# Gated linear attention and two MoE layers on one core: batch row 0 of the attention in three tiles of 128 rows

## The chip, the core and the metric

The kernel runs on one NeuronCore of a Trainium2 chip. What counts is the device time of one launch in microseconds (us), the median of the runs. Engines: PE is TensorE, DVE is VectorE, ACT is ScalarE, POOL is GpSimd, SP is SyncE, which here only issues DMAs. Each engine works through its own list of instructions in order. Line numbers such as L613 are lines of the kernel before; a helper's line stands for everything that it issues.

## The reference, cut to what matters

```
# attention: B, H, S, D = 4, 8, 768, 48
for t in range(S):
    state = alpha[:, :, t, :, None] * state + einsum('bhd,bhe->bhde', k[:, :, t], v[:, :, t])
    y[:, :, t] = einsum('bhd,bhde->bhe', q[:, :, t], state)
x = y.transpose(0, 2, 1, 3).reshape(3072, 384)
# first MoE: the best of 8 experts for each token, 384 -> 1024 (relu) -> 384, times its gate
# second layer for all tokens: 384 -> 2048, h * sigmoid(h), -> 384
```

## The kernel before

The time axis of the attention (768 steps) is cut into 6 chunks of 128. Two heads form a pair; there are 16 pairs `p`, four for each of the 4 batch rows. On chip a pair's q, k and alpha lie with the feature on the partitions: head 0 on partitions 0 to 47, head 1 on 64 to 111, time along the row. Such a layout is a tile. In batch rows 1 to 3 the four pairs share three tiles of 128 partitions: pair `4b + 3` is cut into six pieces of 16 rows, and they lie in the gaps of the other three tiles, on partitions 48 to 63 and 112 to 127 (`ASIDE` says which piece goes where). Batch row 0 instead has four tiles of 112 partitions, one for each pair. So there are 13 tiles `T` (`NTL`).

Each tile is prepared by five steps (`prep`), once for all rows in it:

- `P_SCAN` (L562, output `Pf`): running products of alpha inside each chunk, a scan on DVE, and a small reciprocal (L565).
- `Q_SCALE` (L574): q times `Pf`, on POOL; for tile 0 alone on DVE.
- `DECAY` (L569): copies the chunk ends for the state scan, on ACT.
- `R_SCAN` (L580, output `Rv`): products from the chunk's end backwards, a scan on DVE.
- `K_SCALE` (L585): k times `Rv`, on DVE.

A pair then needs: `scores` (L607) for chunks 0 to 2 and 3 to 5 on PE into the same PSUM tile `Ap`, each half followed by a causal mask that moves it out as `Am` (L613 on DVE, or for some halves a copy on ACT at L626 and two selects on POOL at L630: `beside_scans`); transposes of k (`Tp`, copied to `kst` by ACT at L598); `updates` (L643, L650), which fill `U`; the state scan `So` (L660) on DVE; two copies of it to `Sb` on ACT (L679); and, a pair later, `from_states` (L690) and `within` (L702, L705), which build the output `Yp`, copied out by ACT (L719). The loop over `p` is written so that pair `p` goes with the outputs of pair `p - 1`, and `work` says beside which pair each preparing step stands: `P_SCAN` of a tile stands two pairs before the first pair that uses it, in front of the second half's mask; `R_SCAN` at the end of that same pair; `K_SCALE` at the head of the next. A pair of the kind `4b + 1` has no scans beside it in batch rows 1 to 3.

For the fourth pair of a batch row `gather_last` puts the six pieces together into the extra buffer `E_5` by six DMAs from chip memory to chip memory, issued by POOL. There are five ordinary buffers `E_0` to `E_4` for q and k, three for alpha (`a_`) and four for v.

All input loads are issued by SP. The framework hands out eight counters (`DMAHW0` to `DMAHW7`) in turn to the DMAs of SP and ACT together, and an issue waits until the earlier DMA of its counter has landed. A tile of batch row 0 takes one DMA for each of alpha, q and k; a tile of the others takes four (two of 48 rows, two of 16).

`warm(n)` issues `n` small matmuls of zeros on PE. After the attention the first MoE layer and the second layer follow, both bound by PE; the change does not touch them.

Of the kernel before, what the change touches and what calls it, by code (L numbers as in the profile page):

```python
# [21 lines left out]
B, H, S, D = 4, 8, 768, 48  # L22
NP = B * H // 2
PA = 112
CH = 128
NC = S // CH
SP = NC * (CH + 1)
# [212 lines left out]
def gla_moe_kernel(  # L240
# [12 lines left out]
    nc = tc.nc  # L253
# [151 lines left out]
    with actx:  # L405
# [9 lines left out]


        ASIDE = (((0, 16), (0, 32)), ((1, 0), (1, 16)), ((1, 32), (0, 0)))
        NTL = 4 + 3 * (B - 1)
        NE = 5


        Es = [ac.tile([128, 2 * S + D * NC], F32, name=f"E_{i}") for i in range(NE + 1)]
        tl = {}

        def place(T):
            if T < 4:
                return 0, T
            b, j = divmod(T - 4, 3)
            return b + 1, j

        def parts(e):
            return dict(
# [13 lines left out]
        def load(T, what="aqk"):  # L446
            if T >= NTL:
                return
            b, j = place(T)
            tl.setdefault(T, parts(Es[T % NE]))  # L450
            for x in what:
                src, t = load_to(T, x)
                n = src.shape[2]
                z = src[4 * b + j]
                if b:
                    z = [(0, z[0:D]), (64, z[64:PA])]
                    for i, (h, d) in enumerate(ASIDE[j]):
                        s0 = 64 * h + d
                        z.append((64 * i + D, src[4 * b + 3][s0 : s0 + 16]))
                    for r0, y in z:  # L460
                        nc.sync.dma_start(t[r0 : r0 + y.shape[0]], y)
                else:

                    for c0, c1 in ((0, SP // 2), (SP // 2, n)) if x == "a" and T == 0 else ((0, n),):
                        nc.sync.dma_start(t[0:PA, c0:c1], z[:, c0:c1])

        def load_v(p):
            if p < NP:
# [73 lines left out]
        def gather_last(b):  # L542

            for j in range(3):
                for i, (h, d) in enumerate(ASIDE[j]):
                    s0 = 64 * h + d
                    nc.gpsimd.dma_start(Es[NE][s0 : s0 + 16], Es[(3 * b + 1 + j) % NE][64 * i + D : 64 * i + 64])

        def begin(p):
            b, j = divmod(p, 4)  # L550
            e = Es[p if not b else NE if j == 3 else (3 * b + 1 + j) % NE]
            st.setdefault(p, {}).update(parts(e))

        def prep(T):
            s = tl[T]
            i = T % 2
            n = PA if T < 4 else 128

            def f0():
                s["Pf"] = wk.tile([128, SP], F32, tag="Pf", name="Pf", bufs=3)  # L560
# [58 lines left out]

        def beside_scans(p, g):  # L620

            return (p, g) == (NP - 2, 1) or g == 0 and 1 <= p <= 4

        def mask_aside(p, g):
            m = st[p]["m", g]
# [328 lines left out]
        def f(T, i):  # L954
            if T < NTL:
                if T not in prs:
# [6 lines left out]
        def at(p, place, T, *steps):  # L963
            if T < NTL:
                work.setdefault((p, place), []).extend((T, i) for i in steps)
# [48 lines left out]
        P_SCAN, Q_SCALE, DECAY, R_SCAN, K_SCALE = range(5)  # L1014
        at(0, "head", 1, R_SCAN)
        for T in range(1, NTL):
            b, j = place(T)
            p = 4 * b + j
# [2 lines left out]
                at(p - 2, "scan", T, P_SCAN)  # L1021
                at(p - 2, "end", T, R_SCAN)
        loads = {}
        for T in range(3, NTL):
            b, j = place(T)
            loads[4 * b + j - 3] = T

# [1 line left out]
            for T, i in work.get((p, place), []):  # L1029
                f(T, i)  # L1030

        for i in range(5):
            f(0, i)
        for i in (P_SCAN, Q_SCALE, DECAY):
            f(1, i)
        for p in range(NP + 1):
# [11 lines left out]
            if on:  # L1048
                ks_transpose(p, 0, 3)
                later = []  # L1050
                if beside_scans(p, 0):
                    sooner, *later = mask_aside(p, 0)
                    sooner()
            if p % 4 == 1 and 1 < p < NP:
                gather_last(p // 4)
            prepare(p, "scan")
            aside(p, "F1")
            if 1 <= p <= 4:
                warm(3)
            if oy:  # L1060
                from_states(p - 1, 0)
# [41 lines left out]
            if p == 5:  # L1103
                more_constants()
            aside(p, "C2")
            if 1 <= p <= 3:
                warm(3)
            if not on:
                logits(B - 1)
# [20 lines left out]
    with mctx:  # L1130
# [209 lines left out]
        b = B - 1  # L1340
# [226 lines left out]
        for i in range(0, len(seq), 2):  # L1567
# [18 lines left out]
            for g in (g0, g1):  # L1586
                e, f = divmod(g, NF)
# [11 lines left out]
            e = g0 // NF  # L1599
# [117 lines left out]
```

## Time and profile before

| | before |
|---|---|
| time, median of 3 runs | 756.81 us (755.85 to 757.83) |
| the profiled execution | 757.93 us, of which 755.9 us are the span from the first to the last instruction |
| PE busy | 742.2 us (98%) |
| DVE busy | 466.4 us (62%) |
| ACT busy | 366.5 us (48%) |
| POOL busy | 161.8 us (21%) |

The busy shares are means over unlike stages. The attention takes about the first 147 us; from there on the chain that ended last lies almost wholly on PE. Times below are counted from the start of the span.

### The profile page before, as it was taken

How to read it: one execution, taken by the hardware profiler on the slowest of the kernel's cores; microseconds unless marked ns; L12 is line 12 of the kernel's file. 1: busy time of each engine (PE TensorE's matmuls, PEld its weight loads, DVE VectorE, ACT ScalarE, POOL GpSimd, SP SyncE). 2: the span in 40 equal slices, each digit the busy share in tenths (PEclk: the TensorE clock that was granted, in tenths of full speed). 3: DMA queues.
4: the chain of work that ended last, by engine and by line, in shares of the span. 5: the costliest groups of instructions: out<-in, count | busy, mean ns of one | idle time of the engine just before them, and what ended most of it. 6: DMA issues, size and time to landing. Idle time of an engine off the chain costs nothing.

```text
span 755.9 us, 13462 instructions
## 1 busy us (share of the span) xinstructions
PE 742.2 (98%) x5018; PEld 681.8 (90%) x5018; DVE 466.4 (62%) x779; ACT 366.5 (48%) x685; POOL 161.8 (21%) x206
## 2 busy tenths in 40 slices
PE   8999999999999999999999999999999999999997
PEld 6888888999999999999998999999999999899996
DVE  8999986667787788887786423333342333334222
ACT  2656566445556555656443434544464545334222
POOL 5774321322324223212121200100020010002002
PEclk9999999999999999999999999999999999999999
DMA  9887894445565566653211200030031000001001
GB/s 245 203 208 209 220 287 158 162 131 166 165 201 188 180 207 186 197 181 125 66 40 38 78 19 1 26 90 19 1 100 34 20 22 22 1 1 42 1 0 46
DMA packets 41803, 81.00 MB, mean 107 GB/s; under 512 B 5696, under 2 KB 19999, under 8 KB 41704
## 3 DMA queue, kind: packets, MB, share of 16 engines
q1 hardware_dynamic: 37704, 67.60, 30.7%
q0 software_dynamic: 4000, 12.03, 5.4%
q8 instruction: 68, 1.11, 0.6%
q14 instruction: 31, 0.25, 0.1%
HBM read 68.04 MB, written 9.47 MB: 103 GB/s over the span
## 4 chain that ended last, share of the span: by engine, by line
PE 84%; DVE 6%; issue 4%; ACT 2%; DMA 2%; POOL 1%; POOLq 0%; DVEq 0%; ACTq 0%
PE hp L1238 37%; PE both L1535 12%; PE ob L1535 12%; PE both L1328 9%; PE yb L1328 4%; PE Ap L607 2%; PE Yp L690 1%; PE Lw L535 1%; PE xt L373 1%; PE Yp L705 1%; DMA a__856<-in_alpha_dram 1%; DVE Pf L562 1%; DVE Rv L580 1%; DVE Am L613 1%; ACT Sb L679 1%
## 5 line engine op out<-in xcount | busy, mean ns | idle before, releaser
L1238 PE MATMUL hp<-xh,wh 128*128 128x512 f32 (+10 forms) x498 | 180.0, 364 | 0.4 <-ACT xh L377 0.4
L1238 PE MATMUL hp<-xh,wl 128*128 128x512 f32 (+10 forms) x498 | 179.7, 364 | 0.0
L1512 DVE TENSOR_TENSOR sg<-hp,sg 128x512 f32<-128x512 f32 (+1 forms) x97 | 66.5, 686 | 128.4 <-ACT sg L1511 127.9
L1238 PE MATMUL hp<-xl,wh 128*128 128x512 f32 (+10 forms) x498 | 127.2, 363 | 0.0
L1511 ACT ACTIVATE sg<-hp 128x512 f32<-128x512 f32 (+1 forms) x97 | 57.6, 593 | 118.2 <-PE hp L1238 113.3
L1238 PEld LDWEIGHTS hp<-xh,wh 128*128 128x128 f32 x498 | 93.6, 188 | 11.8 <-issue 0.6
L1238 PEld LDWEIGHTS hp<-xh,wl 128*128 128x128 f32 x498 | 93.6, 188 | 10.6
L1238 PEld LDWEIGHTS hp<-xl,wh 128*128 128x128 f32 x498 | 90.1, 188 | 11.8
L1557 POOL DMA_INDIRECT out_dram<-o,sidx x24 | 23.3, 973 | 275.3 <-ACT o L1555 270.8
L1165 POOL TENSOR_TENSOR wl<-dx,wh 128x384 fp32r<-128x384 f32 x32 | 39.4, 1231 | 166.7 <-ACT wh L1162 166.7
L345 DVE TENSOR_TENSOR wl<-raw,wh 128x768 fp32r<-128x768 f32 x64 | 65.4, 1025 | 7.8 <-ACT wh L341 7.4
L1276 ACT ACTIVATE hh<-hp 128x464 fp32r<-128x464 f32 (+9 forms) x70 | 34.0, 487 | 73.5 <-PE hp L1238 64.1
L1278 DVE SCALAR_TENSOR_TENSOR hl<-hp,hh 128x464 fp32r<-128x464 f32 (+9 forms) x70 | 38.1, 549 | 29.5 <-ACT hh L1276 27.8
L341 ACT CAST wh<-raw 128x768 fp32r<-128x768 f32 x64 | 52.1, 832 | 8.3 <-DMA raw<-in_wt_dram 8.1
L1523 DVE TENSOR_TENSOR hl<-sg,hh 128x512 fp32r<-128x512 f32 x49 | 33.9, 693 | 35.6 <-ACT hh L1522 34.2
L1522 ACT CAST hh<-sg 128x512 fp32r<-128x512 f32 x49 | 30.4, 621 | 49.9 <-DVE sg L1512 38.3
L1523 DVE TENSOR_TENSOR xl<-sg,xh 128x512 fp32r<-128x512 f32 (+1 forms) x48 | 32.7, 682 | 31.7 <-ACT xh L1522 21.3
L1328 PE MATMUL both<-hh,wh 128*128 128x396 f32 (+9 forms) x140 | 47.6, 340 | 0.2 <-ACT hh L1276 0.2
L1328 PE MATMUL both<-hl,wh 128*128 128x396 f32 (+9 forms) x140 | 45.9, 328 | 0.5 <-DVE hl L1278 0.5
L1522 ACT CAST xh<-sg 128x512 fp32r<-128x512 f32 (+1 forms) x48 | 29.3, 611 | 35.1 <-DVE sg L1512 32.8
L1328 PE MATMUL both<-hh,wl 128*128 128x396 f32 (+9 forms) x140 | 45.7, 326 | 0.0
L363 POOL DMA_INDIRECT xg<-x_d,gidx x29 | 32.9, 1136 | 44.7 <-PE xt L373 18.6
(366 smaller groups left out, 1640.6 us busy)
## 6 DMA issues: line engine op xcount, KB each, us to landing
raw<-in_wt_dram SPq DMA_DIRECT2D x64, 384.0 KB
raw<-in_w_dram SPq DMA_DIRECT2D x32, 384.0 KB
raw<-in_alpha_dram SPq DMA_DIRECT2D x16, 336.0 KB
x_d<-xr SPq DMA_DIRECT2D x24, 192.0 KB
E<-in_q_dram SPq DMA_DIRECT2D x18, 144.0 KB
E<-in_k_dram SPq DMA_DIRECT2D x18, 144.0 KB
E<-E POOLq DMA_DIRECT2D x18, 114.0 KB
E<-in_q_dram SPq DMA_DIRECT2D x4, 336.0 KB
```

The lines of the kernel that those rows point to most:

```text
L341: nc.scalar.copy(wslot[slot1(t)][0], raw[t])
L345: eng.tensor_tensor(lo, raw.pop(t), hi.bitcast(F32), op=ALU.subtract)
L1165: nc.gpsimd.tensor_tensor(r["lo"], r["x"], r["hi"].bitcast(F32), op=ALU.subtract)
L1238: nc.tensor.matmul(hp, lhsT=a[:, kc * 128 : (kc + 1) * 128], rhs=x[:, kc, c0:c1], start=(i == 0), stop=(i == 8))
L1276: nc.scalar.activation(hh[:, :n], hp, AF.Relu)
L1278: nc.vector.scalar_tensor_tensor(hl[:, :n], in0=hp, scalar=0.0, in1=hh[:, :n].bitcast(F32), op0=ALU.max, op1=ALU.subtract)
L1328: nc.tensor.matmul(yb[dc][:, c0:c1], lhsT=a[:, c : c + 128], rhs=b_[:, : c1 - c0], start=(f == 0 and c0 == 0 and i == 0), stop=(f == NF - ...
L1511: nc.scalar.activation(sg[:, z], hp[:, z], AF.Sigmoid)
L1512: nc.vector.tensor_tensor(sg[:, z], hp[:, z], sg[:, z], op=ALU.mult)
L1522: nc.scalar.copy(hh[:, z], sg[:, z])
L1523: nc.vector.tensor_tensor(hl[:, z], sg[:, z], hh[:, z].bitcast(F32), op=ALU.subtract)
L1535: nc.tensor.matmul(yb[tt], lhsT=a[:, tt * 128 : (tt + 1) * 128], rhs=b_[:, 384:768], start=(f == 0 and i == 0), stop=(f == NF2 - 1 and i = ...
```

## The change

Batch row 0 is laid out like the others: three tiles of 128 rows, and its fourth pair is gathered by the same six DMAs, issued beside pair 1. There are 12 tiles. The 48-row pieces of all tiles are loaded through SP; the 16-row pieces of tiles 0 and 1 through ACT's queue, those of the others through SP. Tile 0's alpha comes in four 48-row pieces (two column halves) and two of 16 rows. At the head of the program tile 0's `R_SCAN` stands in front of its `Q_SCALE`. The tile that is used from pair 4 on becomes number 3 and is loaded in the opening code, in the place of the fourth pair's tile; no scans stand beside pair 1 any more. The first half's mask of pair 1 moves from ACT and POOL to DVE. Twelve of the small matmuls of `warm` go away: three in the middle of each of pairs 3 and 4, and three at the end of each of pairs 2 and 3. Those beside pair 1 and in the middle of pair 2 stay.

```diff
-        NTL = 4 + 3 * (B - 1)
+        NTL = 3 * B
...
         def place(T):
-            if T < 4:
-                return 0, T
-            b, j = divmod(T - 4, 3)
-            return b + 1, j
+            return divmod(T, 3)
...
                 z = src[4 * b + j]
-                if b:
-                    z = [(0, z[0:D]), (64, z[64:PA])]
-                    for i, (h, d) in enumerate(ASIDE[j]):
-                        s0 = 64 * h + d
-                        z.append((64 * i + D, src[4 * b + 3][s0 : s0 + 16]))
-                    for r0, y in z:
-                        nc.sync.dma_start(t[r0 : r0 + y.shape[0]], y)
-                else:
-
-                    for c0, c1 in ((0, SP // 2), (SP // 2, n)) if x == "a" and T == 0 else ((0, n),):
-                        nc.sync.dma_start(t[0:PA, c0:c1], z[:, c0:c1])
+                for c0, c1 in ((0, SP // 2), (SP // 2, n)) if x == "a" and T == 0 else ((0, n),):
+                    for r0 in (0, 64):
+                        nc.sync.dma_start(t[r0 : r0 + D, c0:c1], z[r0 : r0 + D, c0:c1])
+                for i, (h, d) in enumerate(ASIDE[j]):
+                    s0 = 64 * h + d
+                    (nc.sync if T > 1 else nc.scalar).dma_start(
+                        t[64 * i + D : 64 * i + 64], src[4 * b + 3][s0 : s0 + 16]
+                    )
...
-                    nc.gpsimd.dma_start(Es[NE][s0 : s0 + 16], Es[(3 * b + 1 + j) % NE][64 * i + D : 64 * i + 64])
+                    nc.gpsimd.dma_start(Es[NE][s0 : s0 + 16], Es[(3 * b + j) % NE][64 * i + D : 64 * i + 64])
...
-            e = Es[p if not b else NE if j == 3 else (3 * b + 1 + j) % NE]
+            e = Es[NE if j == 3 else (3 * b + j) % NE]
...
-            n = PA if T < 4 else 128
+            n = 128
...
-            return (p, g) == (NP - 2, 1) or g == 0 and 1 <= p <= 4
+            return (p, g) == (NP - 2, 1) or g == 0 and 2 <= p <= 4
...
-        for T in range(3, NTL):
+        for T in range(4, NTL):
...
-        for i in range(5):
+        for i in (P_SCAN, DECAY, R_SCAN, Q_SCALE, K_SCALE):
             f(0, i)
...
-            if p % 4 == 1 and 1 < p < NP:
+            if p % 4 == 1 and p < NP:
                 gather_last(p // 4)
...
-            if 1 <= p <= 4:
+            if 1 <= p <= 2:
                 warm(3)
...
-            if 1 <= p <= 3:
+            if p == 1:
                 warm(3)
```

The loads of tiles 0 and 1 on SP. Before, from the program's first load to tile 2's alpha (tile 0's alpha is `a__143`, tile 1's `a__148`, tile 2's `a__154`; `E_0` and `E_1` are the q and k of tiles 0 and 1):

```order
L465 DMA a__143<-in_alpha_dram 112x387
L465 DMA a__143<-in_alpha_dram 112x388
L465 DMA E_0_137<-in_q_dram 112x768
L465 DMA E_0_137<-in_k_dram 112x768
L465 DMA a__148<-in_alpha_dram 112x775
L465 DMA E_1_138<-in_q_dram 112x768
L470 DMA v__151<-in_v_dram 128x576
L465 DMA E_1_138<-in_k_dram 112x768
L465 DMA a__154<-in_alpha_dram 112x775 [waits DMAHW0_49]
```

After, on SP from the first load to tile 1's q (tile 1's alpha is now `a__158`):

```order
L454 DMA a__143<-in_alpha_dram 48x387 x2
L454 DMA a__143<-in_alpha_dram 48x388 x2
L454 DMA E_0_137<-in_q_dram 48x768
L454 DMA E_0_137<-in_q_dram 48x768 [waits DMAHW1_49]
L454 DMA E_0_137<-in_k_dram 48x768 [waits DMAHW3_49]
L454 DMA E_0_137<-in_k_dram 48x768 [waits DMAHW5_49]
L454 DMA a__158<-in_alpha_dram 48x775 [waits DMAHW7_49]
L454 DMA a__158<-in_alpha_dram 48x775 [waits DMAHW1_49]
```

Before, the first eight loads wait for nothing and reach to tile 1's k. After, tile 0's second q piece already waits for a counter, and the second piece of tile 1's alpha is the third DMA on counter 1, behind a piece of tile 0's alpha and that q piece. ACT's list now begins with twelve such loads of 16 rows, the last ten of them each behind a counter or another of them, and its first computing instruction stands behind them.

DVE beside pairs 1 and 2. Before, from pair 0's state scan to pair 2's (`So<-U,E_0` is pair 0's, `E_1` pair 1's, `E_2` pair 2's; `Rv` and `Pf` are the scans, a line with `E<-E,Rv` is a `K_SCALE`):

```order
L580 SCALAR_TENSOR_TENSOR Rv_356<-a__154,D1_0_169 112x774 [waits DVE_49]
L585 TENSOR_TENSOR E_2_139<-E_2_139,Rv_356 112x768 [waits DMAHW3_49,DVE_49]
L562 SCALAR_TENSOR_TENSOR Pf_388<-a__160,Z1_166 112x774 [waits DMAHW4_49]
L565 RECIPROCAL D1_1_170<-Pf_388 112x6 [waits DVE_49]
L613 TENSOR_TENSOR Am_414<-Ap_407,mask_173 128x768 [waits PE_49]
L660 SCALAR_TENSOR_TENSOR So_439<-U_199,E_1_138 112x288 [waits PE_49,Activation_49,Pool_49]
L580 SCALAR_TENSOR_TENSOR Rv_446<-a__160,D1_1_170 112x774 [waits DVE_49]
L585 TENSOR_TENSOR E_3_140<-E_3_140,Rv_446 112x768 [waits DMAHW7_49,DVE_49]
L562 SCALAR_TENSOR_TENSOR Pf_483<-a__358,Z1_166 128x774 [waits DMAHW3_49,DMAHW2_49,DMAHW4_49,DMAHW1_49,Pool_49]
L565 RECIPROCAL D1_0_169<-Pf_483 128x6 [waits DVE_49]
L613 TENSOR_TENSOR Am_509<-Ap_502,mask_173 128x768 [waits PE_49]
L660 SCALAR_TENSOR_TENSOR So_534<-U_199,E_2_139 112x288 [waits PE_49,Activation_49]
```

After, the same stretch:

```order
L574 SCALAR_TENSOR_TENSOR Rv_393<-a__173,D1_0_206 128x774 [waits DVE_49]
L607 TENSOR_TENSOR Am_402<-Ap_395,mask_210 128x768 [waits PE_49]
L579 TENSOR_TENSOR E_2_139<-E_2_139,Rv_393 128x768 [waits DMAHW6_49,DMAHW5_49,DMAHW7_49,DMAHW4_49,DVE_49]
L607 TENSOR_TENSOR Am_438<-Ap_431,mask_210 128x768 [waits PE_49]
L654 SCALAR_TENSOR_TENSOR So_462<-U_236,E_1_138 112x288 [waits PE_49,Activation_49,Pool_49]
L556 SCALAR_TENSOR_TENSOR Pf_503<-a__188,Z1_203 128x774 [waits DMAHW2_49,DMAHW3_49,DMAHW1_49,DMAHW0_49]
L559 RECIPROCAL D1_1_207<-Pf_503 128x6 [waits DVE_49]
L607 TENSOR_TENSOR Am_529<-Ap_522,mask_210 128x768 [waits PE_49]
L654 SCALAR_TENSOR_TENSOR So_554<-U_236,E_2_139 112x288 [waits PE_49,Activation_49,Pool_49]
```

Four instructions of the fourth pair's tile are gone (`Pf_388`, its reciprocal, `Rv_446` and the `K_SCALE` on `E_3`), and a mask (`Am_402`) has come in front of tile 2's `K_SCALE`.

POOL beside pair 1, after (`E_5` is the buffer of the gathered pair; before, two selects `Am_378` and tile 3's `Q_SCALE` stood in this place):

```order
L568 TENSOR_TENSOR E_2_139<-E_2_139,Pf_331 128x768 [waits DMAHW1_49,DMAHW2_49,DMAHW0_49,DMAHW7_49,DVE_49,Pool_49]
L541 DMA E_5_142<-E_0_137 16x1824 [waits DMAHW6_49,Activation_49]
L541 DMA E_5_142<-E_0_137 16x1824
L541 DMA E_5_142<-E_1_138 16x1824 [waits DMAHW6_49,Activation_49]
L541 DMA E_5_142<-E_1_138 16x1824
L541 DMA E_5_142<-E_2_139 16x1824 [waits DVE_49,DMAHW6_49,Activation_49,Pool_49]
```

The last pieces wait for DVE, that is for tile 2's `K_SCALE`; a sixth line, the second piece of `E_2`, follows.

## Rows read from the trace of the kernel before

**Rows 1.** The page, busy tenths in 40 slices of 18.9 us.

```profile
DVE  8999986667787788887786423333342333334222
...
PEclk9999999999999999999999999999999999999999
```

**Rows 2.** Timeline of DVE, 3 to 18 us (start, length, instruction, idle before).

```profile
3.33 1.82 DVE L562 TENSOR_TENSOR_SCAN Pf<-a__143,Z 112x387 f32<-112x387 f32 x2 [0.24 <-DMA a__143<-in_alpha_dram]
...
6.26 0.96 DVE L574 TENSOR_TENSOR E<-E,Pf 112x768 f32<-112x768 f32 x1 [0.81 <-DMA E<-in_q_dram]
...
9.81 1.77 DVE L562 TENSOR_TENSOR_SCAN Pf<-a__148,Z 112x774 f32<-112x774 f32 x1
...
17.74 0.92 DVE L613 TENSOR_TENSOR Am<-Ap,mask 128x768 f32<-128x768 f32 x1
```

**Rows 3.** Timeline of DVE, 21 to 32 us.

```profile
21.03 0.96 DVE L585 TENSOR_TENSOR E<-E,Rv 112x768 f32<-112x768 f32 x1
...
21.90 1.76 DVE L562 TENSOR_TENSOR_SCAN Pf<-a__160,Z 112x774 f32<-112x774 f32 x1
...
23.81 0.92 DVE L613 TENSOR_TENSOR Am<-Ap,mask 128x768 f32<-128x768 f32 x1
...
24.64 0.74 DVE L660 TENSOR_TENSOR_SCAN So<-U,E 112x288 f32<-112x288 f32 x1
...
25.31 1.91 DVE L580 TENSOR_TENSOR_SCAN Rv<-a__160,D 112x774 f32<-112x774 f32 x1
...
30.16 0.92 DVE L613 TENSOR_TENSOR Am<-Ap,mask 128x768 f32<-128x768 f32 x1
...
31.00 0.75 DVE L660 TENSOR_TENSOR_SCAN So<-U,E 112x288 f32<-112x288 f32 x1
```

**Rows 4.** Timeline of PE, 11 to 33 us.

```profile
11.00 0.94 PE L607 MATMUL Ap<-E 48*128 48x128 f32 x12
...
14.12 0.94 PE L607 MATMUL Ap<-E 48*128 48x128 f32 x12
...
22.21 0.94 PE L607 MATMUL Ap<-E 48*128 48x128 f32 x12
...
26.96 0.60 PE L690 MATMUL Yp<-E,Sb 112*112 112x128 f32 x4
...
28.64 0.94 PE L607 MATMUL Ap<-E 48*128 48x128 f32 x12
...
31.85 0.94 PE L607 MATMUL Ap<-E 48*128 48x128 f32 x12
```

**Rows 5.** Timeline of ACT, 0 to 29 us.

```profile
0.82 1.28 ACT L569 ACT_TABLE_LOAD   x1 [0.82 <-PEq L1706]
...
25.48 1.27 ACT L679 COPY Sb<-So 48x240 f32<-48x240 f32 x2 [0.55 <-DVE So L660]
...
27.48 0.82 ACT L626 COPY Am<-Ap 128x768 f32<-128x768 f32 x1
```

**Rows 6.** Timeline of the DMA issues of SP.

```profile
1.72 0.42 SPq L465 DMA_DIRECT2D E<-in_q_dram  x1
...
2.65 0.43 SPq L465 DMA_DIRECT2D a__148<-in_alpha_dram  x1
...
8.93 0.31 SPq L465 DMA_DIRECT2D a__160<-in_alpha_dram  x1
```

**Rows 7.** Windows: engines, PEclk, DMA share of 16 engines, GB/s.

```profile
8.00:10.00 2.00, 2.00 (x21) 1.80 (x19) 1.97 (x3) 0.00 (x0) 0.00 (x0) 1.00 1.07 266
```

**Rows 8.** Timelines of POOL and PE around the gather of batch row 1.

```profile
49.05 0.96 POOL L547 DMA_DIRECT2D E<-E  x2 [0.27 <-issue]
...
57.80 1.03 PE L607 MATMUL Ap<-E 48*128 48x128 f32 x12 [0.49 <-DMA E<-E]
```

**Rows 9.** DMA queues, 48 to 50 us: packets, MB, share of 16 engines.

```profile
q0 software_dynamic: 44, 0.19, 66.1%
q1 hardware_dynamic: 60, 0.11, 16.9%
```

## The prediction

> **What bounds the kernel now.** I read the busy shares by slice first. DVE stands at 8 or 9 tenths in the first five slices, to about 95 us, and the granted clock of TensorE is 9 tenths or more everywhere [rows 1]. The change lies in that stretch, so the question is what DVE waits for and who waits for DVE, and the timelines answer it. At the head DVE waits 0.81 us for tile 0's q and for little else [rows 2]. From pair 1 on its instructions follow each other without a gap [rows 3]: pair 1's state scan starts at 24.64, pair 2's at 31.00, a period of 6.36 us. In that time stand one R_SCAN, one K_SCALE, one P_SCAN, a mask and the state scan, and each starts as the one before it ends.
>
> But DVE is not the only tight engine. After a state scan come two copies on ACT (25.48, 1.27 us long) [rows 5], then PE's from_states at 26.96 and the second half's scores at 28.64, which end at 29.58 [rows 4]; only then can DVE mask them, and only then comes the next state scan. The mask starts at 30.16 [rows 3], so DVE is 0.58 us late there. One pair earlier the scores end at 23.15 [rows 4] and the mask starts at 23.81 [rows 3]: 0.66 us late. These small delays, not the length of the scans, are what taking work off DVE can give back. The loop over ACT and PE needs about 5.8 of the 6.36 us whatever DVE does.
>
> **What is removed.** DVE loses the fourth pair's tile: P_SCAN and reciprocal from 21.90 to 23.81, 1.91 us, an R_SCAN like that at 25.31 of 1.91 and a K_SCALE like that at 21.03 of 0.96; it gains a mask of 0.92 [rows 3]. That is 3.86 us less work. If DVE never had to wait, this would be the gain. It will wait, since the removed work stood exactly in front of two masks whose input isn't there yet, and nothing moves into its place.
>
> Pair 1: R_SCAN of tile 2 ends at 21.03, the new mask takes 0.92, K_SCALE 0.87 up to the next start [rows 3], so DVE is free at about 22.8. The second half's scores end at 23.15, after the first half's mask has freed their bank at about 21.95, before PE's 22.21 [rows 4]. The mask therefore starts at about 23.2 instead of 23.81 and the state scan with it: 0.6 us won. Pair 2: PE runs without a gap from 22.21 to 26.96, and the two copies on ACT, 0.6 earlier now, aren't what from_states waits for any more; it still starts near 26.96. What does come earlier is ACT: its copy of the first half's mask ends at 28.30 [rows 5] and may end at 28.0, so the second scores end at 29.2 to 29.3, not 29.58. The mask starts at 29.3 instead of 30.16: **0.9 us won** by the second state scan. The bounds are 0.6 (PE's stretch gives nothing more) and 1.2 (both delays in full, 0.66 + 0.58). Behind that state scan the list is as before, one tile further, with a period that DVE fills, so the 0.9 is neither raised nor lost, and the later stages move as one. The twelve warming matmuls that go lie beside pairs 2 to 4, where PE waits for DVE anyway: nothing, as long as the clock stays up.
>
> **The head.** R_SCAN in front of Q_SCALE hides the 0.81 us of waiting, but this wins nothing by itself: the first mask needs scores that PE starts only at 11.00, behind its warming, and that end at 11.94 [rows 4]. Tile 1's P_SCAN starts at 9.81 [rows 2] and takes 1.91 with its reciprocal, to 11.72, so DVE has 0.2 us to spare there. What counts is when tile 1's alpha is there. Before, this load was issued at 2.65 and had landed by 8.93, when the next issue on its counter went out [rows 6]. Up to its end the rows of the issue list add up to (112 x (775 + 768 + 768 + 775) x 4 bytes =) 1.38 MB; with 128 rows it is 1.58 MB. The 16 DMA engines are full at this time, with 266 GB/s [rows 7], so it can't land before 8.93 + 0.20 / 0.266 = 9.7: no delay, the lower bound. But the second 48-row piece is now third on its counter. The first lands by 3.33; the second, tile 0's q, and the piece itself can each be issued only when the one before has landed. Before, tile 0's q needed from its issue at 1.72 [rows 6] to 6.26, the end of the wait for it [rows 2]: 4.5 us. Two such steps end at 3.33 + 9.0 = 12.3; less 9.81 and the 0.2 to spare this costs 2.3, the upper bound. With at most eight small pieces in flight, 0.6 to 0.8 MB, a step should take 2.3 to 3 us of transfer at 266 GB/s and near 1 us of issue and completion, about 3.5 us: 3.33 + 7.0 = 10.4, 0.6 late. I take **0.4 us lost**, between the bounds by the rate of the full queue. The masks behind it, K_SCALE and the state scan of pair 0 shift with it.
>
> The Trainium skill, "DMA: Bandwidth & Descriptors", speaks against such pieces in its Rules for kernel authors: under 64 KB one pays mostly overhead, and splitting a transfer into partition halves doesn't pay, since both use the same engines. Its section on the anatomy of one DMA gives about 2.0 us fixed plus the bytes at 436 GB/s; by that estimate a piece of 147 KB takes 2.3 us, tile 1's alpha lands near 9 us, the head loses nothing and the sum is 0.4 us lower. This case's 6.3 us for one load in a full queue doesn't agree with a fixed 2 us, so the row decides.
>
> ACT can't compute before its twelve issues are done, the last of them behind tile 1's alpha, so near 11 us; the table load, 1.28 us and now at 0.82 [rows 5], and two decay copies follow. Its copies of transposed k, which stand on PE's way from the first scores at 11.00 to the second at 14.12 [rows 4], then come one to two us later. That is hidden: the second scores end at 15.06 and their mask starts at 17.74 [rows 2], so 2.7 us lie between; without them it would cost its one to two us.
>
> **The gather.** Its six DMAs stand on POOL behind tile 2's Q_SCALE, and the last two wait for tile 2's K_SCALE, which ends near 22.8 + 0.4. They are issued by about 24.2. In batch row 1 the last pair of issues ran from 49.05 to 50.01, and PE's first scores of the gathered pair started at 57.80, after 0.49 us of waiting for the gather [rows 8]: 7.8 us from the last issue. By that, here it ends at 32.0. The scores of pair 3 start at 31.85 now [rows 4]; 0.3 us earlier because of pair 2's second scores and some tenths more because three matmuls in front of them go, say 31.2, plus the 0.4 of the head. PE is 0.4 us late there; its slack of 0.58 towards DVE covers most. I take **0.2 us lost**; bounds 0 (it lands a little sooner) and 1.1 (as late again as 0.4, plus the slack gone). While it runs the gather takes 66% of the DMA engines' time and the loads 17% [rows 9]. The loads of tiles 2 and 3 run beside it now. Tile 3's P_SCAN may be up to 2 us late at no cost, because DVE is idle in front of pair 2's mask. Behind POOL's issues wait only pair 2's selects, due at about 27.5.
>
> **Sum.** 0.4 + 0.2 - 0.9 = -0.3 us against the profiled 757.93, 2.0 us of which lie around the span and don't change. That execution is 1.1 us above the median. Applied to the median of 756.81 this gives 756.5.
>
> **The rivals.**
> 1. *Head in time.* Tile 1's alpha lands by 10.0. Then 0.7 to 0.9 us are won: 756.0. For it: 9.7 is what the bytes alone give. Against: three landings in a row on one counter.
> 2. *Full saving.* DVE's 3.86 us come through, 753.0. This needs PE and ACT to run pair 2 some 3 us faster than now. Against it: PE's stretch from 22.21 to 29.58, of which only single tenths are waiting. For it only that I may misjudge what binds that stretch.
> 3. *Starved head (the other sign).* The eight counters hold too few bytes in flight, so loads fall behind DVE beside pairs 0 and 1. Small pieces with the gather beside them move far less than 266 GB/s: 0.11 MB in 2 us on the loads' queue at worst [rows 9]. Up to tile 2's alpha (3 x 775 + 4 x 768) x 128 x 4 bytes of alpha, q and k and 0.3 MB of v are loaded, 3.06 MB. At 200 GB/s that takes 15.3 us, and with some 2 us of start (the first scan begins at 3.33 [rows 2]) it arrives at 17.3, where its P_SCAN is due at 17.74 - 1.91 = 15.8; later loads add to it. From 3.0 us of delay in these two P_SCANs the kernel is measurably slower: 759.8 at 3.7.
> 4. *Late gather.* If it ends past 32.2 (31.6 + 0.58) the scores of pair 3 hold up its masks and state scan; from 35.0 the kernel is measurably slower, and at 35.5 this costs 3.3 us: 759.6. For it: 7.8 us in batch row 1, with loads less dense than here; against it: the first four pieces are issued two us ahead.
> 5. *Clock.* Without the twelve matmuls, or in a longer pause of PE at the head, the granted clock falls from 2.4 to 1.2 GHz. PE's 5 us in each of pairs 3 and 4 double: 10 us, 766. Against it: the clock stays up after pair 4, where nothing warms [rows 1].
>
> **How the numbers follow.** A change under 0.3%, 2.3 us, can't be told from none here. Chances: the sum above 0.5, head in time 0.2 (both within 0.3%); full saving 0.12; starved head 0.10, late gather 0.06, clock 0.02. So faster 0.12, same 0.70, slower 0.18. The likeliest case's own range, from the bounds (-1.2 with head and gather in time; 2.3 + 0.2 - 0.9 = 1.6 with the head at its upper bound) and the runs' spread of 1 us on either side, is 754.6 to 759.4; the range for 8 in 10 leaves out full saving and most of the slow cases: 754.4 to 759.5.
>
> **What the profile after would show.** DVE idle in front of the second masks of pair 1 (some 0.4 us) and pair 2 (over 2 us); P_SCAN of tile 1 starting at 10 to 10.9 with a wait for a DMA; the table load of ACT at 10 to 11 us; the state scans of pairs 2 and 3 6.3 to 6.4 us apart; PE waiting a few tenths for the gather at pair 3. The prediction is wrong if DVE shows no such idle time (then more is won), if tile 1's or tile 2's alpha comes later than 12 or 19 us, or if state scans from pair 3 on stand over 2 us off their old times.

## The result and the profile after

The kernel after takes 762.03 us (median of 7 executions, 757.76 to 767.35) against 756.81 (755.75 to 757.83, 7 executions): a ratio of 1.0067, with a 95% interval of 1.004 to 1.0094. It is slower by 5.2 us, where 756.5 and "no change" were forecast.

The profiled execution happens to be the quickest of the seven, 757.76 us with a span of 756.0, hardly off the one of before (757.93). The timeline of DVE in it, rows as in [rows 2, 3]:

```profile
4.03 1.82 DVE L556 TENSOR_TENSOR_SCAN Pf<-a__143,Z 128x387 f32<-128x387 f32 x2 [0.93 <-DMA a__143<-in_alpha_dram]
...
10.37 1.77 DVE L556 TENSOR_TENSOR_SCAN Pf<-a__158,Z 128x774 f32<-128x774 f32 x1 [0.61 <-DMA a__158<-in_alpha_dram]
...
19.27 0.75 DVE L654 TENSOR_TENSOR_SCAN So<-U,E 112x288 f32<-112x288 f32 x1
...
24.08 0.96 DVE L607 TENSOR_TENSOR Am<-Ap,mask 128x768 f32<-128x768 f32 x1 [0.41 <-PE Ap L601]
...
30.24 0.96 DVE L607 TENSOR_TENSOR Am<-Ap,mask 128x768 f32<-128x768 f32 x1 [2.65 <-PE Ap L601]
31.12 0.75 DVE L654 TENSOR_TENSOR_SCAN So<-U,E 112x288 f32<-112x288 f32 x1
```

The signs that the prediction asked for are here: tile 1's P_SCAN at 10.37 behind a wait for its alphas, and DVE idle for 0.41 and 2.65 us in front of the second masks of pairs 1 and 2. So are ACT's late table load and the wait of PE behind it (timelines of ACT and PE):

```profile
10.66 1.28 ACT L563 ACT_TABLE_LOAD   x1 [10.66 <-DMA E<-in_k_dram]
```

```profile
13.46 0.41 PE L589 MATMUL Tp<-ident,E 112*128 112x112 f32 x2 [2.21 <-ACT kst L592]
...
32.77 1.03 PE L601 MATMUL Ap<-E 48*128 48x128 f32 x12 [0.67 <-DMA E<-E]
```

This execution shows little of the 5.2 us, so the same kernel was profiled again (run e1_again below: 764.57 us, span 762.9). Its DVE:

```profile
17.47 1.77 DVE L556 TENSOR_TENSOR_SCAN Pf<-a__173,Z 128x774 f32<-128x774 f32 x1 [0.97 <-DMA a__173<-in_alpha_dram]
...
20.22 0.75 DVE L654 TENSOR_TENSOR_SCAN So<-U,E 112x288 f32<-112x288 f32 x1
...
39.34 2.41 DVE L574 TENSOR_TENSOR_SCAN Rv<-a__472,D 128x774 f32<-128x774 f32 x1
...
89.65 2.98 DVE L574 TENSOR_TENSOR_SCAN Rv<-a__1164,D 128x774 f32<-128x774 f32 x1
```

and its POOL:

```profile
38.49 1.63 POOL L568 TENSOR_TENSOR E<-E,Pf 128x768 f32<-128x768 f32 x1 [0.48 <-DMA E<-in_q_dram]
...
45.75 1.63 POOL L568 TENSOR_TENSOR E<-E,Pf 128x768 f32<-128x768 f32 x1 [2.49 <-DMA E<-in_q_dram]
...
89.38 1.63 POOL L568 TENSOR_TENSOR E<-E,Pf 128x768 f32<-128x768 f32 x1 [9.56 <-DVE t L816]
```

Up to the state scan of pair 15 this execution is 5.65 us behind the one of before: 1.65 of them before the first state scan (20.22 against 18.57), 4.0 from there on. Another 1.35 of the 7.0 between the two spans come after it and aren't followed up here. Two things stand out. Loads land late. And R_SCANs, at most 1.91 us long in the loop before [rows 3], take up to 2.98: each stands beside a Q_SCALE of POOL that began just ahead of it, because its queries had come late or POOL was held up by something else. The one of 89.38 ends at 91.01, 1.36 us into the R_SCAN of 89.65, and that R_SCAN is 1.23 us too long. The Trainium skill, "SBUF — State Buffer", Who interferes with whom, says that a VectorE operation with two SBUF inputs and a GpSimd operation that reads SBUF shut each other out, and that the one that starts first holds the port to its end. The trace agrees, with these 1.23 of 1.36 us.

From the state scan of pair 0 to that of pair 15 it needs 107.85 us (before: 103.85). Its ten R_SCANs are together 3.5 us over 1.75 each (before: eleven, 0.6 over), and DVE's waits sum to 12.4 us (before: 7.2), 2.65 of them the idle time forecast for pair 2; the work of one tile less goes the other way.

### The profile page after: what moved, and what is told of

Read it like the earlier page. It is cut to its first block, busy times and chain, and to the rows that moved or that the text cites. A ratio compares the mean times of both kernels' runs of the same rounds, so it can differ in the third digit from the quotient of the medians.

```text
span 756.0 us, 13492 instructions
## 1 busy us (share of the span) xinstructions
PE 742.0 (98%) x5006; PEld 681.4 (90%) x5006; DVE 463.4 (61%) x776; ACT 364.8 (48%) x683; POOL 157.6 (21%) x209
```

## The experiments

Times are medians in us with the number of executions; the ratio is to the kernel before on the same chip. "First" is the start of pair 0's state scan in the profiled execution, "loop" the time from there to that of pair 15 (before: 18.57 and 103.85).

| run | time | before | ratio, 95% interval | first | loop |
|---|---|---|---|---|---|
| e1_again | 762.77 (10) | 758.52 | 1.0045, 1.0025 to 1.0065 | 20.22 | 107.85 |
| e2_sp | 765.81 (4) | 758.52 | 1.0093, 1.0063 to 1.0123 | 21.81 | 106.91 |
| e3_warm | 762.50 (4) | 758.52 | 1.0060, 1.0039 to 1.0081 | 19.95 | 106.41 |
| e4_table | 765.20 (4) | 758.52 | 1.0090, 1.0072 to 1.0108 | 23.55 | 104.93 |
| e5_pieces | 762.58 (7) | 758.15 | 1.0058, 1.0038 to 1.0077 | 19.73 | 110.91 |
| e6_late | 762.41 (8) | 758.15 | 1.0057, 1.0039 to 1.0076 | 19.60 | 108.91 |
| e7_nogather | 763.07 (7) | 758.15 | 1.0060, 1.0038 to 1.0082 | 19.30 | 103.95 |
| e8_half | 764.33 (5) | 758.15 | 1.0083, 1.0052 to 1.0113 | 20.15 | 107.00 |
| e9_whole0 | 758.37 (10) | 758.05 | 0.9997, 0.9970 to 1.0024 | 17.84 | 102.84 |
| e10_whole | 754.27 (10) | 758.05 | 0.9946, 0.9925 to 0.9967 | 17.80 | 101.11 |
| e11_order | 757.84 (10) | 758.05 | 0.9992, 0.9973 to 1.0011 | 18.89 | 102.87 |
| e12_null | 759.08 (10) | 758.05 | 1.0001, 0.9973 to 1.0029 | 19.39 | 104.92 |
| e13_four32 | 764.56 (6) | 757.20 | 1.0095, 1.0062 to 1.0129 | 22.09 | 107.91 |
| e14_before_whole | 756.04 (12) | 757.20 | 0.9979, 0.9965 to 0.9994 | 19.77 | 101.72 |
| e15_whole_again | 753.53 (12) | 757.20 | 0.9955, 0.9938 to 0.9973 | 17.87 | 100.60 |
| e16_pad128 | 755.37 (12) | 756.61 | 0.9980, 0.9967 to 0.9993 | 19.18 | 101.74 |
| e17_whole_third | 753.55 (9) | 756.61 | 0.9959, 0.9942 to 0.9976 | 17.77 | 100.61 |

### First theories: ACT, warming, loads

**e1_again** is the kernel after, unaltered.

> The changed kernel unaltered, to see whether its wide spread (757.8 to 767.4 us in 7 runs, where the kernel before stays within 755.8 to 757.8) comes again on another chip. Theory A (ACT and the clock): ACT stands behind its twelve loads until 10.7 us, PE waits 2.2 us for its first copy of k, the granted clock falls to half for some 3.5 us in the execution whose trace we have, and for longer in others. Then the spread comes again and a slower execution shows a longer or second stretch at half clock, in the first 50 us. Theory B (warming): the missing matmuls beside pairs 2 to 4 let the clock fall there. Theory C (loads): the spread comes from loads that arrive late in varying degree; the clock has no part in it, and DVE shows waits for DMAs of several us. Expected by all three: 758 to 767 us, median about 762; they differ in what a slow trace shows.

This execution of 764.57 us has a mean granted clock of 0.999. The one of 757.76 had stretches at 0.50, the 1.2 GHz level, from 15 to 18 us, behind PE's wait of 2.21 us, and was quicker all the same. Nor do time and mean clock go together over the other executions of this kernel (759.18 us at 0.992, 767.35 at 0.997). The clock is not the cause.

**e2_sp** sends the 16-row pieces of tiles 0 and 1 through SP's queue:

```diff
-                    (nc.sync if T > 1 else nc.scalar).dma_start(
+                    nc.sync.dma_start(
```

> The 16-row pieces of tiles 0 and 1 go through SP like the others, so ACT issues no loads and its table load stands at the start again. Theory A: PE no longer waits 2.2 us at the head, the clock stays at full speed, the spread is gone (runs within 2 us); the head's loads come 1 to 3 us later since SP issues them all, so 757 to 759 us. Theory B and C: the spread stays (C: gets larger, since the loads are later).

It is slower still: DVE waits 2.14 us for the first alphas and 1.33 us for tile 2's. ACT's burden was not the cost; the same pieces cost more in SP's queue.

**e3_warm** brings back the twelve warming matmuls (`1 <= p <= 4` and `1 <= p <= 3`).

> The changed kernel with the twelve warming matmuls of the kernel before put back beside pairs 2 to 4. Theory B: spread gone, 756 to 758 us. Theory A: the fall of the clock at the head stays, but the matmuls put back may shorten the half clock after it; spread mostly stays, median 760 to 763. Theory C: no difference, median 762.

No gain: that term of the prediction, nothing, was right.

**e4_table** puts an activation of one element behind ACT's first two loads, so that the table load stands at 1.75 us and not at 10.66.

> The changed kernel with one tiny activation on ACT right behind its first two loads, so that the table load (1.28 us) is done while the counters are waited for, and no longer stands between the last load and the first copy. Theory A: PE's wait at the head shrinks from 2.2 to about 0.9 us, the clock stays up in most executions, the spread shrinks, 756 to 758 us. Theories B and C: no difference, median 762.

ACT's later loads move back instead, DVE waits 2.34 us for tile 0's queries and 1.33 for its keys, and the time rises. The loads were what mattered.

### What about the loads, and how they reach DVE

**e5_pieces** is the kernel before with only its loads of batch row 0 cut:

```diff
-                        nc.sync.dma_start(t[0:PA, c0:c1], z[:, c0:c1])
+                        for r0, r1 in ((0, D), (64, PA), (D, 64)):
+                            nc.sync.dma_start(t[r0:r1, c0:c1], z[r0:r1, c0:c1])
```

> The kernel before, with each load of batch row 0 cut into rows 0 to 47, 64 to 111 and 48 to 63: 36 whole-tensor pieces in place of 12, as many as the change issues for its three tiles, and nothing else changed. Theory S (small pieces bring the loads in late, and that is what costs): the first 20 us move 215 to 225 GB/s in place of 246, the first state scan starts 0.5 to 3 us after 18.57, and the time is 2 to 5 us above the kernel before. Theory D (the time goes where GpSimd's multiply of the queries and VectorE's reverse scan fall on each other, whatever the pieces): no more than 1 us above, as long as the multiply of the queries starts within 0.4 us of the end of its prefix scan. Rival of both (the layout of three tiles itself costs): no difference.

The pieces alone cost 4.4 us, without any other part of the change: the first 20 us move 188 GB/s, not 246, late alphas cost DVE 2.2 us in the loop, and late queries make long R_SCANs there (2.39 us at 106.14, beside a Q_SCALE that began at 105.27 after 3.27 us of waiting for them). Its profiled execution, 767.07 us, is the slowest of the seven.

**e6_late** is the kernel before with 288 columns copied on POOL ahead of each Q_SCALE from tile 2 on.

> The kernel before, with a copy of 288 columns on GpSimd in front of GpSimd's multiply of the queries of every tile from the third on (768 columns take 1.63 us, so this is an estimated 0.6 us). Theory D: the reverse scan on VectorE starts 1.36 to 1.56 us after that multiply in most tiles and can't run beside it, so each of the eight tiles or so with that spacing has a reverse scan longer by 0.4 to 0.6 us (1.75 to 2.2 or 2.4), the state scans of pairs 0 to 15 spread by 3 to 4.5 us, and the time is 3 to 5 us above the kernel before. Rival (the two engines run side by side and the long scans have another cause): scans of 1.75 to 1.9 us as before, and no difference in time, since GpSimd is idle ahead of most of these multiplies.

The copy takes 0.42 us, and 4.3 us are lost. One pair of it, POOL and then DVE:

```profile
32.26 0.42 POOL L576 COPY late<-Pf 112x288 f32<-112x288 f32 x1
32.65 1.62 POOL L577 TENSOR_TENSOR E<-E,Pf 128x768 f32<-128x768 f32 x1
34.23 0.51 POOL L633 TENSOR_SCALAR_AFFINE_SELECT Am<-Am 128x384 f32<-128x384 f32 x1
```

```profile
33.64 2.73 DVE L583 TENSOR_TENSOR_SCAN Rv<-a__360,D 128x774 f32<-128x774 f32 x1
```

Q_SCALE ends 0.63 us into the R_SCAN, a select of 0.51 follows at once, and the R_SCAN is 0.98 over 1.75. Over the loop the R_SCANs sum to 4.2 us over 1.75 each (0.6 before). A POOL instruction that looks idle-covered costs DVE its lateness.

**e7_nogather** leaves out batch row 0's gather:

```diff
-            e = Es[NE if j == 3 else (3 * b + j) % NE]
+            e = Es[NE if j == 3 and b else (3 * b + min(j, 2)) % NE]
-            if p % 4 == 1 and p < NP:
+            if p % 4 == 1 and 1 < p < NP:
```

> The kernel after, without the gather of batch row 0's fourth pair: pair 3 reads the tile of pair 2 again, so its output is that of other data. Theory G (the gather's 0.7 MB, between 20 and 27 us, push the loads of the tiles behind it back): the multiplies of the queries at 37 to 38 and 44 to 46 us start within 0.4 us of the end of their prefix scans, the reverse scans behind them take under 2.0 us (2.41 and 2.45 in the repeat of the kernel after), the scan that waited 0.4 to 0.7 us for its alphas near 35 us waits no more, and the time is 2 to 3 us under the kernel after, near 760. Theory S (the head's small pieces): under 1 us gained, 762 or more.

In its profiled execution POOL gets its queries in time (timeline of POOL):

```profile
36.33 1.64 POOL L568 TENSOR_TENSOR E<-E,Pf 128x768 f32<-128x768 f32 x1
...
42.69 1.64 POOL L568 TENSOR_TENSOR E<-E,Pf 128x768 f32<-128x768 f32 x1
```

and its R_SCANs sum to 0.3 over 1.75. Its time can't be set beside the others, since the other data are routed differently: from the first pass of ACT over the experts' hidden values to the first one of the last layer it takes 226.1 us, e1_again 222.0. Less these 4.2 it would be 758.9, 3.9 under e1_again. That the gather takes part is likely, but this is one profile and a correction.

**e8_half** splits POOL's Q_SCALE into two halves of 384 columns.

> The kernel after, with GpSimd's multiply of the queries in two halves of 384 columns (an estimated 0.85 us each, from 1.63 for 768), so that a late one holds up the reverse scan by a half at most and the other half runs behind the scan. Theory D: no reverse scan above 2.2 us except where the half is caught at its start (1.75 + 0.8), the sum of what the scans take over 1.75 us falls from 3.5 to under 2 us, and the time is 1 to 2.5 us under the kernel after. Rival (the long scans only stand beside other waits and cost nothing): no difference, 762 to 763.

The long R_SCANs are gone (0.2 us over 1.75 in sum), and nothing is won: the second half now waits behind the R_SCAN, queries are ready later, and DVE waits 8.2 us for scores (5.6 in e1_again). The turn-taking is moved, not removed. Nor does the loss need long R_SCANs: in the loop of e2, e3 and e4 they are together 0.2 to 1.1 us over 1.75, and these runs are 4.0 to 7.3 us slower than the kernel before, with more waiting for alphas, queries and scores. That points to the late loads, and the next runs test it.

### Loads in one piece

For **e9_whole0** the 128 rows of a tile are laid side by side in main memory (a matter of layout, as the padding of the heads is already), and tiles 0 to 2 come in one load per tensor; **e10_whole** does this for all tiles:

```diff
+                z3 = {"q": q3, "k": k3, "a": a3}[x][T]
-                    for r0 in (0, 64):
-                        nc.sync.dma_start(t[r0 : r0 + D, c0:c1], z[r0 : r0 + D, c0:c1])
-                for i, (h, d) in enumerate(ASIDE[j]):
...
+                    nc.sync.dma_start(t[:, c0:c1], z3[:, c0:c1])
```

> The kernel after, with the 128 rows of each tile of batch row 0 laid side by side in main memory, so that queries, keys and alphas of such a tile come in one load each through SyncE's queue (9 loads and one more for the halves of the first alphas, in place of 38; ScalarE issues none); three tiles, gather, masks and order stay. Theory S (the pieces cost): 235 to 250 GB/s in the first 20 us, first state scan at 18 to 19 us (20.22 in the repeat of the kernel after), multiplies of the queries within 0.4 us of their prefix scans up to 50 us, and a time 3 to 6 us under the kernel after, 757 to 760. Theory G (the gather) : the first state scan as early, but late queries and long reverse scans at 37 to 47 us as in the kernel after, and 1 to 2 us gained, 761 to 762. Rival (three tiles themselves cost): 762 to 763.

> As the run with whole loads for batch row 0, but for all four batch rows: 36 loads and one in place of 146. Theory S: late loads and long reverse scans are gone from all pairs, the state scans of pairs 0 to 15 lie 101 to 103 us apart (103.85 before), and the time is under the kernel before, 754 to 757. Rival (the transfers are bound by bytes, not by pieces): as the run with whole loads for batch row 0, within 1 us.

(In e9 the one load stands for T < 3 only.) e9 is level with the kernel before, so the loss is gone, and e10 goes 3.8 us under it. Both keep the gather, and their R_SCANs in the loop are together 0.1 and 0.3 us over 1.75. But the gather lands late where pieces are loaded beside it: at pair 3's first scores PE waits for it in the kernel after (0.67 us), in e1_again (0.89), e3 (2.33) and e9, whose tiles from number 3 on still come in pieces, and not at all in e10, e15 and e17, where all loads are whole. The wait in e9 (PE):

```profile
32.37 1.03 PE L607 MATMUL Ap<-E 48*128 48x128 f32 x12 [1.89 <-DMA E<-E]
```

In the windows from 8 to 20 us, the kernel before, the kernel after and then e15, which is e10 again (PE, PEld, DVE, ACT, POOL, PEclk, DMA share, GB/s):

```profile
8.00:20.00 12.00, 10.86 (x124) 8.99 (x122) 11.69 (x12) 2.63 (x5) 5.47 (x4) 1.00 1.05 270
```

```profile
8.00:20.00 12.00, 9.77 (x96) 7.77 (x93) 11.16 (x13) 3.71 (x6) 6.08 (x6) 0.86 0.92 236
```

```profile
8.00:20.00 12.00, 10.58 (x119) 8.48 (x116) 11.77 (x12) 3.31 (x6) 7.26 (x8) 1.00 1.04 404
```

**e11_order** makes the kernel before run tile 0's R_SCAN ahead of its Q_SCALE; **e12_null** adds to the kernel before a cleared tile of 8 columns that nothing uses.

> The kernel before, with the one part of the change at the head alone: the reverse scan of tile 0 in front of its multiply of the queries. The wait of 0.81 us for the queries at 6.26 us is filled by the reverse scan, so the first state scan starts 0.5 to 0.8 us earlier (18.57 before). If VectorE sets the pace of the next pairs, as the prediction has it, the time falls by 0.3 to 0.8 us; if the head's slack goes into the next wait, no difference within 0.4 us.

> The kernel before, with one more tile of 8 columns on the chip and one clearing of it on GpSimd at the start: a change that does no work that anything waits for. If the 4 to 7 us of the kernels so far come from where tiles lie or from any change at all, this one is 2 us or more above the kernel before too; if they come from the waits that the traces show, it is within 0.5 us of it.

Neither can be told from no change. In e11 the wait for the queries goes, but 0.45 us for keys and 0.42 for tile 1's alphas come in its place: the loads bind, not the order. e12 excludes that any change whatever costs 4 us; its interval reaches from -2.0 to 2.2 us.

**e13_four32** is e9 with each of the whole loads cut into four of 32 rows.

> As the run with whole loads for batch row 0, but each of these loads cut into four of 32 rows, all through SyncE's queue: as many loads and as many bytes in each on average as in the kernel after, none of only 16 rows, none through ScalarE. If the number of loads costs (theory S, by the counters that allow only so many under way or by SyncE's 0.43 us for each issue): 200 to 220 GB/s in the first 20 us, first state scan at 20 us or later, 761 to 765. If the 16-row size or ScalarE's queue costs: 240 GB/s or more, and within 1 us of the run with whole loads, 757.5 to 759.5.

The number of loads on one queue costs, not the 16 rows and not ACT; e2, with its pieces of 48 and 16 rows all in SP's queue, has the same ratio (1.0093). The issues of SP's queue, and a window of the same run:

```profile
0.82 3.63 SPq L459 DMA_DIRECT2D a__143<-in_a_dram  x8
4.50 1.81 SPq L459 DMA_DIRECT2D E<-in_q_dram  x4
6.35 1.81 SPq L459 DMA_DIRECT2D E<-in_k_dram  x4
```

```profile
2.00:12.00 10.00, 9.07 (x70) 7.21 (x68) 6.76 (x10) 0.73 (x2) 4.79 (x20) 1.00 0.67 173
```

The queue issues without a pause, 0.45 us for each, and the DMA engines are busy for only two thirds of the time: 98 KB in 0.45 us are 217 GB/s at most, and the first alphas' halves of 48 KB half of that.

The kernel after is near this limit from tile 2 on, whose four pieces for each tensor SP issues alone. Its queue (timeline of SP):

```profile
5.43 1.19 SPq L454 DMA_DIRECT2D a__158<-in_alpha_dram  x2
...
11.33 0.78 SPq L454 DMA_DIRECT2D a__173<-in_alpha_dram  x2
12.15 0.93 SPq L457 DMA_DIRECT2D a__173<-in_alpha_dram  x2
...
20.87 0.88 SPq L457 DMA_DIRECT2D E<-in_q_dram  x2
```

From 11.33 to 21.75 it issues 21 loads almost without a pause. Ahead of that, up to 11.33, it issues 15 and stands still for some 3.6 us, waiting for earlier loads. Pieces can also be moved more slowly by themselves: in e5, from 8 to 20 us, the DMA engines are busy throughout (share 1.04) and move 221 GB/s, where the kernel before moves 270. How the loss divides between issuing, counters and this is not separated.

**e14_before_whole** is the kernel before with batch rows 1 to 3 whole; **e16_pad128** loads also its four tiles of batch row 0 as 128 rows, the last 16 padding. **e15_whole_again** and **e17_whole_third** are e10 on the same two chips.

> The kernel before, four tiles for batch row 0 as they are, with batch rows 1 to 3 loaded whole, one load of 128 rows for each tensor of a tile. Beside the run with whole loads everywhere it prices the change itself, without pieces. If three tiles for batch row 0 and the new order at its head are worth what the traces say (first state scan 0.8 us earlier, pairs 0 to 3 apart 17.7 in place of 18.8 us): 1 to 2.5 us above that run, 755.5 to 757.5. If the pieces were all and three tiles are worth nothing: within 0.7 us of it, 754 to 755.

> The run with whole loads for all batch rows once more, on the chip of the run before with whole loads: 753 to 756, under the kernel before by 0.3 to 0.8 per cent. If it is not under it, its first result was chance.

> The kernel before with whole loads for batch rows 1 to 3, and the four tiles of batch row 0 loaded as 128 rows too, of which the last 16 are padding that nothing reads: 14 per cent more bytes for these tiles, four tiles as before. If loads of 112 rows are moved slower than loads of 128 (250 to 300 GB/s in the traces with tiles of 112 rows, 390 to 430 with tiles of 128, the transfer engines over nine tenths busy in both), the first 10 to 20 us move 380 to 420 GB/s, the first state scan starts at 18.2 to 18.8 us (19.77 without), and the time is 754.5 to 755.5, so that about half of the 2.5 us between the four tiles and the three with whole loads are the loads' and not the tiles'. If the rate is set by something else, the first state scan stays at 19 us or later and the time at 755.5 to 757.

> The kernel after with whole loads for all batch rows, beside the padded four tiles on the same chip: 753 to 755. What is left between the two is what three tiles are worth by themselves: 1 to 2 us if the pairs 0 to 3 keep the 1.1 us that the traces show there.

e15 is 2.5 us under e14, e17 1.8 us under e16. The padding wins nothing measurable by itself (ratios 0.9979 and 0.9980, on two chips), and three tiles keep 1.8 us over four padded ones, so the rate of the 112-row loads isn't what separates four tiles from three. With whole loads everywhere the change makes the kernel faster; with whole loads for batch row 0 alone (e9) it is level. In the profiled executions of e16 and e17, 2.9 us apart, the head gives 1.4 us (19.18 to 17.77; e16 waits 1.31 us for tile 0's queries at 6.86) and the loop 1.1 (101.74 to 100.61), all of it in the first three pairs: 18.83 us from the first state scan to the fourth against 17.72. DVE of e16 at the wait, then of e17 in the first pairs:

```profile
6.86 0.96 DVE L573 TENSOR_TENSOR E<-E,Pf 112x768 f32<-112x768 f32 x1 [1.31 <-DMA E<-in_q_dram]
```

```profile
22.39 0.96 DVE L613 TENSOR_TENSOR Am<-Ap,mask 128x768 f32<-128x768 f32 x1 [0.48 <-PE Ap L607]
23.27 0.74 DVE L660 TENSOR_TENSOR_SCAN So<-U,E 112x288 f32<-112x288 f32 x1
...
28.56 0.96 DVE L613 TENSOR_TENSOR Am<-Ap,mask 128x768 f32<-128x768 f32 x1 [2.66 <-PE Ap L607]
29.43 0.75 DVE L660 TENSOR_TENSOR_SCAN So<-U,E 112x288 f32<-112x288 f32 x1
```

## Why the prediction was wrong

- **What bounds the kernel** (DVE by its chain, with PE close behind): right, but a third party was left out. An R_SCAN of DVE keeps its length of 1.75 to 1.91 us only as long as POOL's Q_SCALE is over, or nearly so, when it begins, and that hangs on the queries' landing.
- **The loop's gain, 0.9 by pair 2's state scan (bounds 0.6 to 1.2):** right in size. From the first state scan to the third e16 needs 12.43 us and e17 11.66, 0.77 less; even in e1_again it is 0.79 less than before.
- **The step that failed:** "the list is as before, one tile further, with a period that DVE fills, so the 0.9 is neither raised nor lost, and the later stages move as one". From the third state scan, 31.00 [rows 3] and 31.86, to the sixteenth the kernel before needs 91.42 us and e1_again 96.21, 4.8 more (the quick first execution 92.18). Already pairs 2 and 3 are 6.82 us apart in e1_again, not 6.3 to 6.4. The list is the same, but its loads are not: they run late behind the head's pieces (e5, e9), and the gather beside pieces lands late too. In the sum the loads were priced at one place only, tile 1's alphas. The sixteenth state scan, before and in e1_again:

```profile
122.42 0.76 DVE L660 TENSOR_TENSOR_SCAN So<-U,E 112x288 f32<-112x288 f32 x1 [1.59 <-PE U L650]
```

```profile
128.07 0.76 DVE L654 TENSOR_TENSOR_SCAN So<-U,E 112x288 f32<-112x288 f32 x1 [1.08 <-PE U L644]
```

- **The head, 0.4 lost (0 to 2.3):** mis-sized within its bounds, 0.7 in the first execution and 1.65 in e1_again. The working's 10.4 for tile 1's P_SCAN was right (10.37 and 10.14), and its alphas cost 0.61 and 0.27 us of waiting; more came from the first alphas, now in six pieces (first scan at 4.03, not 3.33), and from tile 2's (0.97). For tile 1's alphas the counters that the working relied on were the smaller part: their last issue ends at 6.62, not 3.08; five more issues of 0.45 us make 2.3 of this, standing still the other 1.3. The working had issuing only as a part of "near 1 us" in each step, not summed over the pieces. Without pieces the head gains 1.4, so "this wins nothing by itself" for R_SCAN's new place holds only while loads hold up what follows it (e11).
- **ACT one to two us late, hidden:** about right. PE waits 2.21 us for ACT's copy of keys, but pair 0's second scores still end at 16.02, and their mask starts at 18.44, behind other work of DVE and no wait.
- **The gather, 0.2 lost (0 to 1.1):** its landing was about rightly priced (PE waits 0.67 us). That its transfers run among the loads of tiles 2 and 3 was said and not priced; e7 speaks for a cost there, uncertain in size. The 1.1 that bounded the landing is not a bound beside pieces: PE waits 2.33 us in e3 and 1.89 in e9.
- **Warming, nothing:** right (e3).
- **The rivals.** The starved head, given 0.10 and 759.8, was the right mechanism at too small a price: its 17.3 for tile 2's alphas is what e1_again shows (17.47), but it was followed to them alone and not to POOL and the later pairs.
- **Luck.** The profiled execution, 757.76, lies inside the forecast range, though it too loses at the head and late queries hold up two of its Q_SCALEs; it is one end of a spread of 9.6 us.
- **The weighing of the rule.** The Trainium skill, "DMA: Bandwidth & Descriptors", speaks in its Rules for kernel authors against small pieces and partition halves, and the prediction let its row decide on one load's landing time. That decision was right for tile 1's alphas: the fit of 2.0 us that the prediction took from the same page is one for DMAs that GpSimd issues, and by it two steps after 3.33 end at 8.0 (not "near 9"), where 10.14 and 10.37 were measured. The runs bear the rule out: e5 is 4.4 us over its kernel before by pieces alone, and e13 7.4 over it where e9 is level.

What stays open: why executions of the same kernel after differ by up to 9.6 us. The two profiles differ in which Q_SCALE meets which R_SCAN. On one chip the spread shrinks as loads gain room (754.53 to 760.56 in 20 executions before, 754.78 to 755.80 in 12 of e16), which fits late loads; but e9 still reaches from 754.39 to 761.26, and once 767.30, so it is not shown.

## What to carry to other kernels

Price a load by the queue that issues it, not only by its bytes: where pieces x issue time is longer than the time in which the DMA engines move the same bytes, as in e13, later stages that live on prefetch are late. When two engines share a resource, a chain without gaps on the one is a fact about the other's timing, so ask of each change whether it moves the other's start. And follow a late load past the place where it first waits: here 1.65 us lost at the head stood beside 4.8 us later.

## What the runs showed of the hardware that was not expected

- An R_SCAN on DVE and a Q_SCALE on POOL shut each other out both ways: R_SCAN 2.98 us in place of 1.75 when POOL is first, Q_SCALE 3.76 us in place of 1.63 when DVE is first, here with a state scan and the R_SCAN behind it (both in e1_again; the second in the line below). The lost time shows as a longer instruction, not as idle time, so no view of waits has it.

```profile
73.09 3.76 POOL L568 TENSOR_TENSOR E<-E,Pf 128x768 f32<-128x768 f32 x1 [6.08 <-DVE Am L607]
```

- Where most loads have 112 rows 270 GB/s are moved (8 to 20 us in the kernel before), with loads of 128 rows 404 (e15), with the DMA share at 1.05 and 1.04. Sixteen rows of padding made the first 20 us move 331 GB/s, not 242 (e16, e14), but the first state scan came only 0.6 us earlier, since tile 0's queries still came late. The Trainium skill, "SBUF — State Buffer", Door 1, has the rate hang on how many of the 16 ports the partitions reach and asks for all 128 rows in one transfer. The runs agree with the second; the count of ports doesn't explain it, since by that section's table partitions 0 to 111 reach all 16 too, four of them by half. Why the rates differ stays open; a busy share near 1 at both tells nothing of it. The two windows, e14 and then e16:

```profile
0.00:20.00 20.00, 14.51 (x139) 11.68 (x139) 15.78 (x20) 3.82 (x6) 10.22 (x32) 1.00 0.93 242
```

```profile
0.00:20.00 20.00, 16.43 (x148) 12.99 (x149) 16.37 (x21) 3.81 (x6) 10.90 (x32) 1.00 0.90 331
```

- One issue on SP's queue takes 0.45 us when it never waits (e13), and about the same, 0.42 to 0.43, for a whole load of 344 KB [rows 6], so 98 KB a piece caps a queue at 217 GB/s.
